# Sums of x for the seven products formed at an attention pair's end, weights kept as float32, and the second half's groups in opposite order

## The chip, the cores and the metric

One core of one Trainium2 chip runs the whole program. The metric is the device time of one execution in microseconds (us); the number shown for a kernel is the median of its runs. The granted clock is the TensorE clock that the profile shows for a stretch, as a fraction of 2.4 GHz.

## The reference

Causal attention for 4 batches and 12 heads (448 positions, head dimension 64), and then a two-layer network on its output, with a squared ReLU between the layers:

```
scores = q @ k.T / sqrt(64); masked above the diagonal; softmax; @ v    # per batch and head
x = attention output as 1792 rows (4 batches x 448) of 768 columns
h = max(x @ w_in, 0)            # 768 x 2048
out = (h * h) @ w_out           # 2048 x 768
```

q, k and v come as float32, the two weights as 64-bit floats.

## The kernel before

**Numbers.** TensorE works on float32 operands in its reduced form, so each operand is kept as two tiles, a high part and a low part (the rest after the high part is taken away), and each product is three matmuls: high x high, high x low, low x high. `split` makes the two parts: a copy for the high part (POOL or ACT, L299) and a subtraction for the low part (DVE or POOL, L301). A weight arrives as 64-bit words; `piece` (L497) loads 128 rows into one of three `raw` buffers, builds the float32 value in one of three `z` buffers (two steps on ACT, three on DVE), and splits it into `wi_t` (w_in) or `late["wo"]` (w_out).

**Stages.** Attention runs in 24 pairs of heads. Pairs 0 to 11 (batches 0 and 1) come first, and their results are split straight into `x_t`. Then the network runs on these 896 rows; meanwhile pairs 12 to 23 (batches 2 and 3) go through attention one after the other on the `a` buffers, and each result goes from PSUM to a buffer of pool `r` and on to DRAM (`x_dram`, L460 to L467). The second half of the network then works on batches 2 and 3.

**The network.** The 2048 columns of w_in come in `NG` = 4 groups. Per group: an h stretch (x times the group's part of w_in, ReLU, square, split into `g_t`) and an o stretch (g times the group's part of w_out), in which 14 output tiles are added up over the groups in `acc` (L764 to L769) and written out in the last group (L770). In the first half the h stretch is done directly (`h_unit`). Each group's two weight parts are also stored, both of the split parts, in DRAM (`keep`, L477: `wi_split`, two stores per row block; `wo_split`), for use in the second half.

**The second half** does each h stretch with seven products in place of eight (`h_pair`, L681). x and w are seen as 2 x 2 blocks. The x side needs, for each of three row blocks i, x11, x21, x22 and the sums t1 = x12 - x11, t2 = x22 - t1, t3 = x22 - x12 and t4 = x21 - t2; x11 and x21 are the two column halves of batch 2, x12 and x22 those of batch 3. `x_parts` (L589) loads the four blocks of one i from `x_dram` into four buffers of pool `f` (L594), makes the four sums with `combine` (DVE or POOL, L287 or L291), and splits all seven results into 21 tiles (L599 to L600). Nine of these tiles lie where attention's buffers were (free at `attended`), twelve in `x_t` (free at `entered`, when the first half's last h stretch is done). They are handed out i by i, while the products take them in the order of `SEVEN`: x11 of i = 0, 1, 2, then t2 of i = 0, 1, 2, then x21, t3, t1, t4, x22.

The w side (`w_parts`, L622) fetches, for each half u of a group, the split parts of three blocks and adds them to whole values (`whole`, L635 or L637), fetches the two parts of the fourth and adds them (L658), makes four sums (`made`), and splits these (`done`). The three blocks that need no sum are used as fetched. Each group's w_out parts come back with `fetch` (L490), eight loads of 384 KB that write the high and low tiles directly.

**What sets the order.** `Plan` is a list scheduler that runs when the program is built. Each operation has a rank, one or more ways (an engine, an estimated duration, the instruction), operations it needs, and the buffers it takes and gives back. `emit` (L97) steps through a simulated time: of all operations that are ready and whose buffer is free, it issues the one that can start first, and the rank only breaks ties; where an operation has several ways it takes the engine on which it would end first. All engines get their instructions in that planned order and execute them in order, SP's DMA issues too. So every wait on the chip is where the chip differs from the plan.

Of the kernel before, what the change touches and what calls it, by code (L numbers as in the profile page):

```python
# [163 lines left out]
def kernel(  # L164
# [17 lines left out]
    nc = tc.nc  # L182
# [73 lines left out]
    plan.pool("r", tiles("r", NR, [P, S], F32), r=2, xs=2, y=6)  # L256
    plan.pool("f", [], fz=5, s=3, xp=4)
# [50 lines left out]
    def attention(s, n, at):  # L308
# [144 lines left out]
        if n < NA:  # L453
            x = x_t[n]
            plan.op(at, [on_act(S, lambda: x[:, 0], lambda: av.t[:, :S], True)],
                    [av], [(("x", n), 0)])
            plan.op(at, [on_dve(S, lambda: x[:, 1], lambda: av.t[:, :S],
                                lambda: x[:, 0].bitcast(F32), ALU.subtract)],
                    [av, (("x", n), 0)], [(("x", n), 1)], drop=[av])
        else:  # L460
            xs = Hold("r", "xs")
# [4 lines left out]
            plan.op(at, [(DMA, 0.7, lambda: nc.sync.dma_start(out=x_dram[n - NA], in_=xs.t))],  # L466
                    [xs], [("xd", n - NA)], drop=[xs])  # L467

# [3 lines left out]
    wo_dram = nc.dram_tensor("wo_split", (NG, 2 * GF, P, 2, CH), F32, kind="Internal").ap()  # L472

    def wo_part(a, ch):
        return late["wo"][:, :, a, ch * CH:(ch + 1) * CH].bitcast(F32)

    def keep(rank, kind, gr, a, ch, after):  # L477
        if kind == "i":
            def go():
                for i in range(2):  # L480
                    nc.sync.dma_start(
                        out=wi_dram[gr, :, a // CB, :, i, a % CB].rearrange("f p n -> p f n"),
                        in_=wi_t[:, i, a].bitcast(F32).rearrange("p (f n) -> p f n", n=P))
            plan.op(rank, [(DMA, 1.9, go)], [(("wi", a), 0), (("wi", a), 1)], [("wid", gr, a)], after)
            return
        plan.op(rank, [(DMA, 1.7, lambda: nc.sync.dma_start(
            out=wo_dram[gr, a + GF * ch], in_=wo_part(a, ch)))],
            [(("wo", a, ch), 0), (("wo", a, ch), 1)], [("wod", gr, a, ch)])

    def fetch(rank, gr, a, ch):  # L490
        plan.op(rank, [(DMA, 1.7, lambda: nc.sync.dma_start(
            out=wo_part(a, ch), in_=wo_dram[gr, a + GF * ch]))],
            [("wod", gr, a, ch)], [(("wo", a, ch), 0), (("wo", a, ch), 1)])
# [3 lines left out]
    def piece(rank, kind, gr, a, ch, after):  # L497
# [40 lines left out]
        split(rank, n, lambda: dst(0), lambda: dst(1), zf, [zt], key, after, [zt])  # L538
        pieces.extend(plan.ops[mark:])
# [41 lines left out]
    x7, owned = {}, {}  # L581
# [7 lines left out]
    def x_parts(i, rank, after):  # L589

        B = {}
        for m, (key, n) in enumerate((("11", i), ("12", NP + i), ("22", NP + CB + i), ("21", CB + i))):
            B[key] = h = Hold("f", "xp")
            plan.op(rank - 6 + m, [(DMA, 0.9, lambda h=h, n=n: nc.sync.dma_start(out=h.t, in_=x_dram[n]))],  # L594
                    [("xd", n)], [h], take=h)

        def done(key):
            t = x7[key, i]
            split(rank, S, lambda: t()[:, 0], lambda: t()[:, 1], lambda: B[key].t, [B[key]],  # L599
                  ("x7", key, i), [after[owned[key, i]]], [B[key]])  # L600
        B["t1"], B["t2"] = Hold("r", "xs"), Hold("r", "xs")
        combine(rank, S, B["t1"], B["12"], B["11"], ALU.subtract, [B["12"], B["11"]], [B["t1"]],
                after=[attended], take=B["t1"], drop=[B["11"]])
        done("11")
        combine(rank, S, B["t2"], B["22"], B["t1"], ALU.subtract, [B["22"], B["t1"]], [B["t2"]],
                take=B["t2"], drop=[B["t1"], B["22"]])
        done("t2")
        done("21")
        B["t3"] = B["12"]
        combine(rank, S, B["12"], B["22"], B["12"], ALU.subtract, [B["22"]], [B["12"]],  # L610
                drop=[B["22"]])
        done("t3")
        done("t1")
        B["t4"] = B["21"]
        combine(rank, S, B["21"], B["21"], B["t2"], ALU.subtract, [B["t2"]], [B["21"]],
                drop=[B["t2"]])
        done("t4")
        done("22")
# [3 lines left out]
    def w_parts(gr, u, rank, last):  # L622
# [22 lines left out]
        for m, (key, f, j) in enumerate((("11", 0, 0), ("22", 1, 1), ("12", 0, 1))):  # L645
            W[key] = w = Hold("w", "w")
            r, src, saved = fetched(m, f, j)
            plan.op(r, [(DMA, 1.2, lambda w=w, src=src: nc.sync.dma_start(out=w.t.bitcast(F32), in_=src))],
                    saved, [(w, 0), (w, 1)], gate, take=w)
            whole(key, lambda w=w: flat(w.t[:, 0].bitcast(F32)), lambda w=w: flat(w.t[:, 1].bitcast(F32)),  # L650
                  [(w, 0), (w, 1)], [w])
        pair = [Hold("f", "fz"), Hold("f", "fz")]
        r, src, saved = fetched(3, 1, 0)
        for i, h in enumerate(pair):
            plan.op(r, [(DMA, 0.7, lambda h=h, i=i: nc.sync.dma_start(
                out=h.t[:, :CBW].rearrange("p (c n) -> p c n", n=P), in_=src[:, i]))], saved, [h], gate, take=h)
        Z["21"] = pair[0]
        combine(rank, CBW, pair[0], pair[0], pair[1], ALU.add, [pair[1]], [pair[0]], drop=[pair[1]])  # L658
# [8 lines left out]
        def made(key, a, b, op, drop):  # L667
            combine(rank, CBW, Z[key], Z[a], Z[b], op, [Z[a], Z[b]], [Z[key]],
                    take=Z[key] if key != "s3" else None, drop=[Z[d] for d in drop])
        made("s1", "21", "22", ALU.add, ("22",))  # L670
        made("s2", "s1", "11", ALU.subtract, ("s1", "11"))
        done("s2")
        made("s3", "11", "21", ALU.subtract, ("11",))
        done("s3")
        done("s1")
        made("s4", "12", "s2", ALU.subtract, ("12", "s2"))
# [63 lines left out]
    def o_unit(ph, gr, t, ch, rank, step, after):  # L740
# [23 lines left out]
        if gr == 0:  # L764
# [4 lines left out]
        plan.op(rank, ways, [ps], [("acc", t, ch)], after if gr == 0 else (), drop=[ps])  # L769
        if gr == NG - 1:  # L770
# [80 lines left out]
    keys = [(key, i) for key in ("11", "t2", "21", "t3", "t1", "t4", "22") for i in range(CB)]  # L851
    for i, key in enumerate(sorted(keys, key=lambda k: k[1])):
        x7[key] = ((lambda i=i: late["x"][i]) if i < NX else (lambda i=i: x_t[i - NX]))
        owned[key] = i >= NX
    for i in range(CB):
        x_parts(i, begin + (rank - begin) * (i + 0.5) / CB, [attended, entered])
    for ph in range(1, NPH):
        for gr in range(NG):
            begin, rank = group(ph, gr, rank, 1.0, begin)
# [33 lines left out]
```

## Time and profile before

| | |
|---|---|
| median of 3 runs | 632.28 us (631.47 to 632.42) |
| the profiled execution's own time | 631.39 us |
| its span, first to last instruction | 629.6 us |
| granted clock, mean | 0.989 |
| busy: TensorE / POOL / DVE / ACT | 604.6 / 371.8 / 367.3 / 325.2 us |
| moved by DMA | 103.77 MB, mean 165 GB/s |

The profiled execution is 1.8 us longer than its span, which is what lies before the first and after the last instruction. A matmul's record is longer than the distance to the next one, because matmuls are pipelined, so TensorE's busy time says where it idled but not how fast it went; for that the granted clock and the number of matmuls in a stretch are needed. Engines other than TensorE cost time only where TensorE waits for them.

### The profile page before, as it was taken

The numbers are of one execution on the slowest core, as the hardware profiler recorded it, in microseconds if no ns is written. First come the engines' busy times: TensorE is split into PE (matmuls) and PEld (weight loads), VectorE is DVE, ScalarE is ACT, GpSimd is POOL, SyncE is SP. The second block draws the span as 40 slices with busy tenths as digits, with TensorE's granted clock in tenths as the row PEclk, the third lists the DMA queues.
The fourth block names the chain that finished last, engine by engine and source line by source line (L and its number), as shares of the span: only waits on it lengthen the run. The fifth ranks groups of instructions, "written<-read, shape, count | busy, mean of one in ns | idle before, by whom it ended". The sixth has DMA issues, their size and how long they took to land.

```text
span 629.6 us, 11242 instructions
## 1 busy us (share of the span) xinstructions
PE 604.6 (96%) x3864; PEld 532.2 (85%) x3864; DVE 367.3 (58%) x822; ACT 325.2 (52%) x803; POOL 371.8 (59%) x454
## 2 busy tenths in 40 slices
PE   4989999999999899999999999799999999999997
PEld 2656677898888798898898889799999999999997
DVE  5679976386767788767874219944015424533222
ACT  4679896865687646587556433345235003302400
POOL 2456766644767763787846459989238706914510
PEclk9799999999999899999999999999999999999999
DMA  9877852797897899886964144873234234333022
GB/s 146 164 187 132 180 122 56 170 324 260 217 258 227 230 256 275 228 251 177 257 199 156 50 129 154 280 223 101 100 110 141 82 126 145 101 101 102 1 89 87
DMA packets 175225, 103.77 MB, mean 165 GB/s; under 512 B 115264, under 2 KB 164928, under 8 KB 175168
## 3 DMA queue, kind: packets, MB, share of 16 engines
q1 hardware_dynamic: 171456, 102.59, 58.9%
q10 hardware_dynamic: 3712, 0.46, 0.5%
q8 instruction: 30, 0.49, 0.3%
q14 instruction: 27, 0.22, 0.1%
HBM read 69.60 MB, written 33.42 MB: 164 GB/s over the span
## 4 chain that ended last, share of the span: by engine, by line
PE 60%; DVE 4%; issue 1%; DMA 1%; POOL 0%; ACT 0%; DVEq 0%; ACTq 0%
PE ps L754 9%; PE ps L756 9%; PE ps L755 9%; PE ps L693 5%; PE ps L695 5%; PE ps L697 5%; PE ps L559 3%; PE ps L561 3%; PE ps L560 3%; PE ps L417 2%; PE ps L397 2%; PE ps L357 2%; DVE x L287 1%; DVE acc L287 1%; DVE words L287 1%
## 5 line engine op out<-in xcount | busy, mean ns | idle before, releaser
L756 PE MATMUL ps<-wo,g 128*128 128x384 f32 x448 | 150.4, 336 | 2.5 <-POOL g L291 2.5
L754 PE MATMUL ps<-wo,g 128*128 128x384 f32 x448 | 152.4, 340 | 0.0
L755 PE MATMUL ps<-wo,g 128*128 128x384 f32 x448 | 150.3, 336 | 0.0
L383 POOL TENSOR_SCALAR ap<-ap,asm 128x64 f32<-128x64 f32 (+6 forms) x120 | 73.9, 636 | 43.6 <-DVE asm L442 22.2
L287 DVE TENSOR_TENSOR acc<-ps,acc 128x384 f32<-128x384 f32 x84 | 46.1, 553 | 84.1 <-PE ps L756 70.5
L284 ACT ACTIVATE r<-ps 128x448 f32<-128x448 f32 x60 | 32.8, 546 | 107.5 <-PE ps L697 79.3
L756 PEld LDWEIGHTS ps<-wo,g 128*128 128x128 f32 x448 | 84.4, 188 | 2.8 <-POOL g L291 2.8
L754 PEld LDWEIGHTS ps<-wo,g 128*128 128x128 f32 x448 | 84.5, 189 | 1.3 <-issue 0.8
L370 DVE CUSTOM_DVE_ANT_0 ps<-ps,mask 128x448 f32<-128x448 f32 (+6 forms) x168 | 68.7, 443 | 27.5 <-PE ps L357 18.3
L755 PEld LDWEIGHTS ps<-wo,g 128*128 128x128 f32 x448 | 84.6, 189 | 0.2
L284 ACT ACTIVATE words<-words 128x384 f32<-128x384 f32 (+3 forms) x112 | 64.5, 614 | 25.7 <-DMA words<-in_moe_w_in_dram 8.6
L559 PE MATMUL ps<-x,wi 128*128 128x448 f32 x192 | 74.4, 387 | 0.3 <-DVE x L287 0.3
L561 PE MATMUL ps<-x,wi 128*128 128x448 f32 x192 | 70.3, 366 | 0.9 <-POOL wi L291 0.9
L560 PE MATMUL ps<-x,wi 128*128 128x448 f32 x192 | 70.2, 365 | 0.0
L374 ACT ACTIVATE ap<-ps,mx 128x448 f32<-128x448 f32 (+6 forms) x126 | 58.7, 483 | 21.3 <-DVE mx L370 15.6
L287 DVE TENSOR_TENSOR r<-ps,r 128x448 f32<-128x448 f32 x40 | 24.9, 623 | 73.7 <-PE ps L697 71.1
L294 POOL TENSOR_SCALAR wi<-words 128x512 fp32r<-128x512 f32 (+1 forms) x27 | 15.9, 589 | 85.1 <-PE ps L695 57.2
L291 POOL TENSOR_TENSOR g<-r,g 128x448 fp32r<-128x448 f32 x50 | 59.5, 1195 | 5.5 <-ACT g L284 2.7
L284 ACT ACTIVATE r<-r 128x448 f32<-128x448 f32 x76 | 43.9, 577 | 21.8 <-DVE r L287 20.4
L693 PE MATMUL ps<-x,wi 128*128 128x448 f32 x138 | 51.3, 372 | 3.7 <-ACT r L284 3.7
L291 POOL TENSOR_TENSOR wi<-words,wi 128x512 fp32r<-128x512 f32 (+1 forms) x41 | 52.3, 1279 | 1.7
L695 PE MATMUL ps<-x,wi 128*128 128x448 f32 x138 | 51.2, 371 | 0.0
(94 smaller groups left out, 1157.4 us busy)
## 6 DMA issues: line engine op xcount, KB each, us to landing
words<-in_moe_w_in_dram SPq DMA_DIRECT2D x24, 512.0 KB, 4.8
words<-in_moe_w_out_dram SPq DMA_DIRECT2D x32, 384.0 KB, 4.1
wi_split<-wi SPq DMA_DIRECT2D x48, 256.0 KB, 3.6
wo_split<-wo SPq DMA_DIRECT2D x32, 384.0 KB, 3.9
wo<-wo_split SPq DMA_DIRECT2D x32, 384.0 KB, 5.1
wi<-wi_split SPq DMA_DIRECT2D x18, 384.0 KB, 3.5
out_dram<-acc SPq DMA_DIRECT2D x28, 192.0 KB, 1.9
v<-in_v_dram SPq DMA_DIRECT2D x24, 192.0 KB, 4.6
```

The lines of the kernel that those rows point to most:

```text
L284: return (ACT, t_act(n, psum, more), lambda: nc.scalar.activation(dst(), src(), func, **kw))
L287: return (DVE, t_dve(n) + more, lambda: nc.vector.tensor_tensor(out=dst(), in0=a(), in1=b(), op=op))
L291: lambda: nc.gpsimd.tensor_tensor(out=dst(), in0=a(), in1=b(), op=op))
L383: (POOL, 0.0005 * CW[c] + 0.34, lambda: nc.gpsimd.tensor_scalar(*operands(), 1.0, op0=ALU.mult, op1=ALU.mult)),
L559: nc.tensor.matmul(o, w[:, 0], x[:, 0], start=c == 0, stop=False)
L560: nc.tensor.matmul(o, w[:, 0], x[:, 1], start=False, stop=False)
L561: nc.tensor.matmul(o, w[:, 1], x[:, 0], start=False, stop=c == NP - 1)
L693: nc.tensor.matmul(o, w.t[:, 0, c], x[:, 0], start=begin and c == 0, stop=False, skip_group_check=True)
L695: nc.tensor.matmul(o, w.t[:, 0, c], x[:, 1], start=False, stop=False, skip_group_check=True)
L754: nc.tensor.matmul(res(), g[:, 0], w[:, 0], start=f == 0, stop=False)
L755: nc.tensor.matmul(res(), g[:, 0], w[:, 1], start=False, stop=False)
L756: nc.tensor.matmul(res(), g[:, 1], w[:, 0], start=False, stop=f == GF - 1)
```

## The change

Four things change together.

1. The sums t1 to t4 are no longer made in `x_parts` from blocks loaded back. A new function `spill` is called when a pair's attention ends. For batch 3 it has loaded the earlier blocks ahead of time into buffers of pool `r` (kind `xs`, now 4 of them), and subtracts them from the attention result while that is still in PSUM: t1 for the first three column blocks; t2, t3 and t4 for the other three. The sums are stored in a new DRAM tensor `xt_dram`. As before, x itself is stored too.
2. `x_part` takes the place of `x_parts`: each of the 21 tiles is one load (three buffers of kind `xp`, before four) and one split, and the tiles are handed out in the order in which the products take them.
3. The second half takes the groups in the order 3, 2, 1, 0. Group 3's w_out parts are still in place from the first half, so nothing is fetched for them. Its outputs are added up in that order and written out with group 0.
4. Weights are kept as float32. `piece` stores the `z` buffer itself: w_out of groups 0 to 2 (196 KB in place of 393 KB each), w_in of groups 1 to 3 (`wz_dram`). The split parts of w_in are kept for groups 0 and 3 alone. `fetch` now loads into a buffer of kind `fo` and splits. `w_parts` differs by group: group 0 as before; group 3 fetches the split parts of the three direct blocks and, beside them, four float32 blocks for its sums; groups 1 and 2 fetch four float32 blocks and split three of them for direct use.

```diff
-    plan.pool("r", tiles("r", NR, [P, S], F32), r=2, xs=2, y=6)
-    plan.pool("f", [], fz=5, s=3, xp=4)
+    plan.pool("r", tiles("r", NR, [P, S], F32), r=2, xs=4, y=6)
+    plan.pool("f", [], fz=5, s=3, xp=3, fo=2)
...
+    def spill(n, av, at):
+        b, c = divmod(n, NP)
+        gate, mark = list(last_sums), len(plan.ops)
...
+        def loaded(place, key):
+            h = Hold("r", "xs")
+            plan.op(at - 8, [(DMA, 0.9, lambda: nc.sync.dma_start(out=h.t, in_=place))],
+                    [key], [h], gate, take=h)
+            return h
+        def less(h, drop):
+            plan.op(at, [(DVE, t_dve(S) + 0.05, lambda: nc.vector.tensor_tensor(
+                out=h.t, in0=result(), in1=h.t, op=ALU.subtract))], [av], [h], drop=drop)
...
+        if second and c < CB:
+            h = loaded(x_dram[c], ("xd", c))
+            less(h, [av])
+            stored(h, *t_place(1))
+        elif second:
+            t1 = loaded(*t_place(1))
+            x21 = loaded(x_dram[c], ("xd", c))
+            x12 = loaded(x_dram[n - CB], ("xd", n - CB))
+            less(t1, [av])
             plan.op(at, [
-                on_act(S, lambda: xs.t, lambda: av.t[:, :S], True),
-                (DVE, t_dve(S) + 0.05, lambda: nc.vector.tensor_copy(xs.t, av.t[:, :S])),
-            ], [av], [xs], take=xs, drop=[av])
...
+                (DVE, t_dve(S) + 0.4, lambda: nc.vector.tensor_tensor(
+                    out=x21.t, in0=x21.t, in1=t1.t, op=ALU.subtract)),
+                (POOL, t_pool(S, True), lambda: nc.gpsimd.tensor_tensor(
+                    out=x21.t, in0=x21.t, in1=t1.t, op=ALU.subtract))], [t1], [x21])
+            less(x12, [av])
+            stored(t1, *t_place(2))
+            stored(x12, *t_place(3))
+            stored(x21, *t_place(4))
+        xs = Hold("r", "xs")
+        plan.op(at, [
+            on_act(S, lambda: xs.t, result, True),
+            (DVE, t_dve(S) + 0.05, lambda: nc.vector.tensor_copy(xs.t, result())),
+        ], [av], [xs], take=xs, drop=[av])
+        last_sums[:] = plan.ops[mark:]
+        stored(xs, x_dram[n], ("xd", n))
...
     def fetch(rank, gr, a, ch):
-        plan.op(rank, [(DMA, 1.7, lambda: nc.sync.dma_start(
-            out=wo_part(a, ch), in_=wo_dram[gr, a + GF * ch]))],
-            [("wod", gr, a, ch)], [(("wo", a, ch), 0), (("wo", a, ch), 1)])
+        h = Hold("f", "fo")
+        plan.op(rank - 6, [(DMA, 0.9, lambda: nc.sync.dma_start(
+            out=h.t[:, :CH], in_=wo_dram[gr, a + GF * ch]))], [("wod", gr, a, ch)], [h], take=h)
+        cols = slice(ch * CH, (ch + 1) * CH)
+        split(rank - 2, CH, lambda: late["wo"][:, 0, a, cols], lambda: late["wo"][:, 1, a, cols],
+              lambda: h.t[:, :CH], [h], ("wo", a, ch), drop=[h])
...
         split(rank, n, lambda: dst(0), lambda: dst(1), zf, [zt], key, after, [zt])
+        if kind == "o" and gr < NG - 1:
+            plan.op(rank, [(DMA, 0.8, lambda: nc.sync.dma_start(out=wo_dram[gr, a + GF * ch], in_=zf()))],
+                    [zt], [("wod", gr, a, ch)], drop=[zt])
+        if kind == "i" and gr > 0:
+            plan.op(rank, [(DMA, 1.0, lambda: nc.sync.dma_start(
+                out=wz_dram[gr, :, a // CB, :, a % CB].rearrange("f p n -> p f n"),
+                in_=zf().rearrange("p (f n) -> p f n", n=P)))],
+                [zt], [("wzd", gr, a)], drop=[zt])
...
-    def x_parts(i, rank, after):
...
+    def x_part(key, i, rank, after):
+        t, h = x7[key, i], Hold("f", "xp")
+        if key[0] == "t":
+            k = int(key[1])
+            place, saved = xt_dram[k - 1, i], ("xt", k, i)
+        else:
+            n = {"11": 0, "21": CB, "22": NP + CB}[key] + i
+            place, saved = x_dram[n], ("xd", n)
+        plan.op(rank - 4, [(DMA, 0.9, lambda: nc.sync.dma_start(out=h.t, in_=place))], [saved], [h], take=h)
+        split(rank, S, lambda: t()[:, 0], lambda: t()[:, 1], lambda: h.t, [h], ("x7", key, i), [after], [h])
...
-        for m, (key, f, j) in enumerate((("11", 0, 0), ("22", 1, 1), ("12", 0, 1))):
+        for m, (key, f, j) in enumerate((("11", 0, 0), ("12", 0, 1), ("22", 1, 1))):
+            if gr not in (0, NG - 1):
+                continue
...
+            if gr == 0:
+                whole(key, lambda w=w: flat(w.t[:, 0].bitcast(F32)), lambda w=w: flat(w.t[:, 1].bitcast(F32)),
+                      [(w, 0), (w, 1)], [w])
...
+        else:
+            for m, (key, f, j) in enumerate((("21", 1, 0), ("22", 1, 1), ("11", 0, 0), ("12", 0, 1))):
+                Z[key] = h = Hold("f", "fz")
+                plan.op(rank - 10 + m, [(DMA, 0.7, lambda h=h, f=f, j=j: nc.sync.dma_start(
+                    out=h.t[:, :CBW].rearrange("p (c n) -> p c n", n=P), in_=wz_dram[gr, 2 * u + f, j]))],
+                    [("wzd", gr, CB * j + c) for c in range(CB)], [h], gate, take=h)
...
+        def direct(key):
+            if gr not in (0, NG - 1):
+                done(key)
...
                 piece(at, "i", gr, c, 0, ())
-                keep(at + 4, "i", gr, c, 0, swap)
+                if gr in (0, NG - 1):
+                    keep(at + 4, gr, c, swap)
...
                 piece(at, "o", gr, i % GF, i // GF, swap)
-                keep(at + 2, "o", gr, i % GF, i // GF, ())
-            else:
+            elif gr < NG - 1:
                 fetch(at, gr, i % GF, i // GF)
...
-    keys = [(key, i) for key in ("11", "t2", "21", "t3", "t1", "t4", "22") for i in range(CB)]
-    for i, key in enumerate(sorted(keys, key=lambda k: k[1])):
...
+    keys = [(OTHER[key], i) for key in SEVEN for i in range(CB)]
+    for m, key in enumerate(keys):
+        x7[key] = ((lambda m=m: late["x"][m]) if m < NX else (lambda m=m: x_t[m - NX]))
+        x_part(*key, begin + (rank - begin) * (m + 0.5) / len(keys), attended if m < NX else entered)
     for ph in range(1, NPH):
-        for gr in range(NG):
+        for gr in range(NG - 1, -1, -1):
             begin, rank = group(ph, gr, rank, 1.0, begin)
```

## Rows read from the trace of the kernel before

**Rows 1.** Engines by stretch, whole span: length, busy us (instructions), clock, DMA.

```profile
0.00:100.00 100.00, 85.68 (x724) 57.44 (x726) 78.32 (x258) 78.54 (x236) 55.33 (x102) 0.97 0.78 153
100.00:371.50 271.50, 268.08 (x1801) 233.35 (x1797) 179.18 (x415) 173.20 (x432) 170.34 (x209) 0.99 0.74 209
371.50:401.30 29.80, 29.80 (x173) 29.75 (x172) 26.55 (x29) 10.59 (x22) 27.92 (x22) 1.00 0.61 201
401.30:412.00 10.70, 7.03 (x27) 5.98 (x26) 10.21 (x12) 4.50 (x10) 9.42 (x8) 0.84 0.73 225
412.00:629.60 217.60, 214.02 (x1149) 205.65 (x1147) 73.02 (x110) 58.36 (x108) 108.76 (x116) 1.00 0.34 107
```

**Rows 2.** TensorE's waits, whole span: us in total, times, longest us.

```profile
PE ps L693 <- ACT r L284: 3.7, 1, 3.7
...
PE ps L756 <- POOL g L291: 2.5, 1, 2.5
...
PE ps L561 <- POOL wi L291: 0.9, 1, 0.9
```

**Rows 3.** The stretches around the second half's first products, as rows 1.

```profile
404.55:408.18 3.63, 0.00 (x0) 0.00 (x0) 3.63 (x4) 1.51 (x5) 3.52 (x4) 1.00 0.82 229
408.18:411.80 3.62, 3.62 (x10) 3.22 (x11) 3.33 (x4) 1.21 (x3) 2.45 (x3) 0.54 0.59 200
411.80:420.00 8.20, 8.20 (x41) 7.53 (x41) 3.12 (x5) 4.59 (x10) 7.89 (x10) 1.00 0.92 273
```

**Rows 4.** ACT in order of time: start us, us, ... [idle before <-releaser].

```profile
406.71 0.58 ACT L284 ACTIVATE x<-r 128x448 fp32r<-128x448 f32 x1 [2.12 <-DVE r L287]
...
407.61 0.52 ACT L284 ACTIVATE r<-ps 128x448 f32<-128x448 f32 x1
```

**Rows 5.** The stretches around TensorE's first-half wait, as rows 1.

```profile
210.30:212.80 2.50, 0.06 (x1) 0.00 (x0) 1.50 (x3) 1.89 (x4) 2.50 (x3) 1.00 0.97 340
212.80:217.20 4.40, 4.36 (x21) 4.25 (x21) 2.65 (x5) 2.22 (x4) 1.67 (x2) 0.62 0.91 261
```

**Rows 6.** Groups by form, 372 to 412 us: xcount, busy us, mean ns, idle.

```profile
L287 DVE TENSOR_TENSOR x<-words,x 128x448 fp32r<-128x448 f32 x9 | 10.7, 1215 | 0.0
...
L637 POOL TENSOR_TENSOR words<-wi 128x384 f32<-128x384 f32 x4 | 5.2, 1304 | 0.0
...
L637 POOL TENSOR_TENSOR words<-w 128x384 f32<-128x384 f32 x2 | 2.8, 1398 | 0.0
...
L287 DVE TENSOR_TENSOR r<-words 128x448 f32<-128x448 f32 x2 | 2.2, 1096 | 0.0
...
L287 DVE TENSOR_TENSOR words<-words 128x448 f32<-128x448 f32 x1 | 1.6, 1571 | 0.0
```

**Rows 7.** Loads of x_dram (L594, 12 in the whole span).

```profile
L594 SPq DMA_DIRECT2D words<-x_dram x12: 372/426/600, 343.2 to 400.2; - x12
...
DMA to landing us min/median/max: 2.5/3.3/5.5
```

**Rows 8.** Group of instructions, the page, whole span: DVE adding from PSUM.

```profile
L287 DVE TENSOR_TENSOR r<-ps,r 128x448 f32<-128x448 f32 x40 | 24.9, 623 | 73.7 <-PE ps L697 71.1
```

**Rows 9.** One 128x512 piece: z taken on ACT, ready and last read on DVE.

```profile
201.38 0.67 ACT L284 ACTIVATE words<-words 128x512 f32<-128x512 f32 x1
...
208.28 0.85 DVE L535 SCALAR_TENSOR_TENSOR words<-words 128x512 int32<-128x512 int32 x1
...
210.42 0.68 DVE L287 TENSOR_TENSOR wi<-words,wi 128x512 fp32r<-128x512 f32 x1
```

**Rows 10.** DMA issues, 120 to 330 us: KB each, median us to landing.

```profile
wo_split<-wo SPq DMA_DIRECT2D x28, 384.0 KB, 4.1
words<-in_moe_w_out_dram SPq DMA_DIRECT2D x26, 384.0 KB, 4.2
words<-in_moe_w_in_dram SPq DMA_DIRECT2D x18, 512.0 KB, 4.6
```

**Rows 11.** DVE's L287 in the second half, 425 to 600 us: ns min/median/max.

```profile
L287 DVE TENSOR_TENSOR words<-words x8: 548/962/1368, 427.1 to 553.5; 128x384 f32<-128x384 f32 x8
```

More of the change, by code (lines that the diff above doesn't have):

```diff
@@ L460, in attention @@
         else:
[L461 to L467 removed]
+            spill(n - NA, av, at)
+    xt_dram = nc.dram_tensor("xt_dram", (4, CB, P, S), F32, kind="Internal").ap()
@@ new lines, with result, stored, t_place @@
+    last_sums = []
+    def spill(n, av, at):
+        b, c = divmod(n, NP)
+        gate, mark = list(last_sums), len(plan.ops)
+        def result():
+            return av.t[:, :S]
+        def stored(h, place, key):
+            plan.op(at, [(DMA, 0.7, lambda: nc.sync.dma_start(out=place, in_=h.t))], [h], [key], drop=[h])
+        def loaded(place, key):
[6 more added lines that the diff above has]
+                out=h.t, in0=result(), in1=h.t, op=ALU.subtract))], [av], [h], drop=drop)
+        def t_place(k):
+            return xt_dram[k - 1, c % CB], ("xt", k, c % CB)
+        second = b == 1
+        if second and c < CB:
[7 more added lines that the diff above has]
+            less(t1, [av])
+            plan.op(at, [
+                (DVE, t_dve(S) + 0.4, lambda: nc.vector.tensor_tensor(
[13 more added lines that the diff above has]
+        stored(xs, x_dram[n], ("xd", n))
@@ L490, in fetch, with keep, go @@
-    def fetch(rank, gr, a, ch):
-        plan.op(rank, [(DMA, 1.7, lambda: nc.sync.dma_start(
-            out=wo_part(a, ch), in_=wo_dram[gr, a + GF * ch]))],
-            [("wod", gr, a, ch)], [(("wo", a, ch), 0), (("wo", a, ch), 1)])
+    wo_dram = nc.dram_tensor("wo_whole", (NG, 2 * GF, P, CH), F32, kind="Internal").ap()
+    wz_dram = nc.dram_tensor("wi_whole", (NG, GF, 2, P, CB, P), F32, kind="Internal").ap()
+    def keep(rank, gr, a, after):
+        def go():
+            for i in range(2):
+                nc.sync.dma_start(
+                    out=wi_dram[gr, :, a // CB, :, i, a % CB].rearrange("f p n -> p f n"),
+                    in_=wi_t[:, i, a].bitcast(F32).rearrange("p (f n) -> p f n", n=P))
+        plan.op(rank, [(DMA, 1.9, go)], [(("wi", a), 0), (("wi", a), 1)], [("wid", gr, a)], after)
@@ L649, in w_parts @@
                     saved, [(w, 0), (w, 1)], gate, take=w)
[L650 to L658, printed above, removed]
+            if gr == 0:
+                whole(key, lambda w=w: flat(w.t[:, 0].bitcast(F32)), lambda w=w: flat(w.t[:, 1].bitcast(F32)),
+                      [(w, 0), (w, 1)], [w])
+        if gr == 0:
+            pair = [Hold("f", "fz"), Hold("f", "fz")]
+            r, src, saved = fetched(3, 1, 0)
+            for i, h in enumerate(pair):
+                plan.op(r, [(DMA, 0.7, lambda h=h, i=i: nc.sync.dma_start(
+                    out=h.t[:, :CBW].rearrange("p (c n) -> p c n", n=P), in_=src[:, i]))], saved, [h], gate, take=h)
+            Z["21"] = pair[0]
+            combine(rank, CBW, pair[0], pair[0], pair[1], ALU.add, [pair[1]], [pair[0]], drop=[pair[1]])
+        else:
[4 more added lines that the diff above has]
+                    [("wzd", gr, CB * j + c) for c in range(CB)], [h], gate, take=h)
         Z["s1"], Z["s2"], Z["s4"] = Hold("f", "s"), Hold("f", "s"), Hold("f", "s")
@@ L763, in o_unit @@
             rank += step
-        if gr == 0:
+        first, final = (0, NG - 1) if ph == 0 else (NG - 1, 0)
+        if gr == first:
             ways = [on_act(CH, acc, res, True),
@@ L768, in o_unit @@
             ways = [on_dve(CH, acc, res, acc, ALU.add)]
-        plan.op(rank, ways, [ps], [("acc", t, ch)], after if gr == 0 else (), drop=[ps])
-        if gr == NG - 1:
+        plan.op(rank, ways, [ps], [("acc", t, ch)], after if gr == first else (), drop=[ps])
+        if gr == final:
             rows = slice(ph * T + t * P, ph * T + (t + 1) * P)
```

50 lines of the change are left out of this document (4 added, 46 removed).

## The prediction, made before the result was known

> **What bounds the kernel now.** I read the stretches of the span first, then TensorE's waits, then the one place that the change aims at.
>
> By stretch [rows 1] TensorE is busy all but 14.3 us of the first 100 us, all but 3.4 us of the next 271.5, all of the 29.8 us of the last o stretch of the first half, 7.03 of the next 10.7 us, and then all but 3.6 us to the end, which are the tail after the last matmul. DVE and POOL are far from full in the second half (73.0 and 108.8 of 217.6 us). So TensorE's own work is the bound, and only its idle time and its slow clock can be won. After the first 100 us, whose order the change hardly touches, TensorE waits three times [rows 2]: 3.7 us for ACT at the second half's start, 2.5 us for POOL in the first half, 0.9 us for POOL.
>
> The first wait is at the hand-over [rows 3]. From 404.55 to 408.18 no matmul runs. From 408.18 to 411.80 the granted clock is 0.54, nearly all at 1.2 GHz, and 10 matmuls take 3.62 us; from 411.80 41 of them take 8.20 us, 0.20 us each, at 2.4 GHz. So the wait costs 3.63 us and the clock behind it 10 x (0.362 - 0.200) = 1.6 us: 5.2 us together.
>
> What TensorE waits for is ACT's copy of the first product out of PSUM at 407.61. ACT works in order, and ahead of the copy it stood 2.12 us for DVE's sum of x whose high part it makes at 406.71 [rows 4]; the copy could have run when the product was done. The sums t1 to t4 of the last row block are what is late. The two engines that make them are full: in the 40.5 us from 371.5 to 412 DVE and POOL are busy 26.55 + 27.92 + 10.21 + 9.42 = 74.1 of 81.0 us [rows 1].
>
> The second wait shows the same price elsewhere [rows 5]: 2.5 us idle, then 4.40 us at a clock of 0.62, which loses 4.40 x 0.38 = 1.7 us: 4.2 us.
>
> **The change, part by part.**
>
> *Sums leave the hand-over.* Twelve sums stand there, seven on DVE and five on POOL; the shortest form takes 1.096 and the longest 1.571 us [rows 6]. At the middle, 1.33, they are 16.0 us (13.2 to 18.9). They go.
>
> *Group 3 first.* Its float32 blocks need no high-plus-low sum: of these, six on POOL cost 5.2 + 2.8 = 8.0 us in this stretch [rows 6], and two pair sums at the same 1.3 us cost 2.6 us. Eight loads of w_out parts leave SP's queue and the DMA engines there too. Together DVE and POOL lose 26.6 of 74.1 us; 47.5 us are left, 24 us for each of two engines, so their work could end at about 371.5 + 24 = 395.5, before the products begin at 401.3. The tiles also come in the order of use: the first product needs three tiles, where before x11 of the last block was made last.
>
> *x loads.* All 21 tiles now come by a load, through three buffers. The buffers are to be had well before 371.5, since the first load of x stands at 343.2 [rows 7], so three are full when the places of the tiles come free at 371.5. Eighteen follow in six rounds. A round is a load of 3.3 us (2.5 to 5.5), an issue of 0.43 us [rows 7], a high part of about 0.57 us (the ACT row at 406.71 shows 0.58) and a low part of 1.2 us (DVE's mean in this stretch [rows 6]): 5.5 us. The tiles are wanted at 401.3 + 0.2 x 3 x m for the m-th of 21, the last at about 413.5. The first three are worked off by some 374, and 374 + 6 x 5.5 = 407. That leaves 6.5 us. With every load at its longest, 5.5 us, and low parts at the 1.57 of the longest form, a round is 8.1 us and the last tile comes at 422.6, 9 us late. I take no wait, because the median row is nearest to how the loads stand, and keep 9 us as the other end.
>
> *Sums at a pair's end.* Nine subtractions read PSUM and one buffer. The nearest row is DVE adding from PSUM, 0.623 us, in 40 cases [rows 8]: 5.6 us, and three sums of the old kind, 4 us. DVE is busy 179 of 271.5 us there [rows 1]; this lies beside TensorE. The subtraction adds a wait on DVE for its loaded operand, and queued behind it on DVE are the additions into acc and attention's maxima, for which TensorE waits through its PSUM banks. But these loads may go as soon as the pair before is done, and twelve pairs share 271.5 us, so about 20 us ahead of use against a landing of at most 5.5 us [rows 7]. Nothing, and if the cover goes, the difference.
>
> *DMAs of the first half.* SP issues 24 more for the sums (12 loads, 12 stores), 6 fewer for w_in (48 become 24 + 18) and 8 fewer for w_out: 10 more at 0.43 us, 4.3 us in 271.5. In bytes, split w_in loses 6.3 MB, w_out 7.9 MB, float32 w_in adds 4.7 MB and the sums 5.5 MB: 4.0 MB less, while the DMA engines are busy 0.74 of this stretch [rows 1]. I count neither a gain nor a loss; a gain is not excluded.
>
> *z buffers.* A store now reads z, so z comes free only when the store has landed. One piece holds z from 201.38 to 211.10, 9.7 us [rows 9]. The nearest store, w_out's split parts, lands in 4.1 us at twice the size [rows 10]; begun when the value is ready, at 209.1, it lands some 2.5 us after the old release: 12.2 us. Three buffers give a piece each 210 / 44 x 3 = 14.3 us (26 + 18 loads in 210 us [rows 10]). It fits by 2 us on average; queued behind the wait on ACT are ReLU copies and exponentials, with TensorE behind them through two banks. I take nothing, and a stall like that of [rows 5], 4.2 us, as the other end.
>
> *Second half.* Twenty-four w_out blocks are split again: 24 copies on ACT or POOL and 24 subtractions on DVE or POOL. By the row of DVE's subtractions and sums of this size, 0.55 to 1.37 us, median 0.96 [rows 11], these are 23 us on engines busy half the time or less [rows 1]; w_parts adds two operations per half of groups 1 and 2 (8) and saves as many in group 3 beyond the hand-over. It is needed one o stretch ahead, so nothing on the path. The spread of that row, 0.55 to 1.37 for one shape, shows that DVE is slowed when POOL works too. The Trainium skill (SBUF — State Buffer, section "SBUF: two separate sides") says that a DVE operation with two SBUF inputs and a GpSimd operation hold a shared port pair by turns, each for its whole length. By that rule the two engines' work adds up, 181.8 of 217.6 us now and about 205 with the change, which would leave few gaps; what this gives is the third rival.
>
> *The sum.* 631.39 - 3.63 - 1.6 = 626.2 for an execution like the profiled one, which stands 0.9 us under the median of 632.28. Set against the median: **627.0 us**.
>
> **The rivals.**
>
> 1. *The loads of x set the pace* (slower side). For: SP's queue is in order, with stores of outputs that wait for DVE between the loads, and only three buffers. It begins to cost when a round is over (413.5 - 374) / 6 = 6.6 us, and decides, so that the whole gain of 5.2 us is gone, at about 7.2 us: late by 3.6 us, and 1.6 us for the clock behind it. At 8.1 us a round it gives 627.0 + 9 + 1.6 = 637.6. Against: the median load gives 5.5.
> 2. *The first-half wait goes too.* The order from 100 us on is planned anew, DMA is lighter, and POOL's wait need not come back: 627.0 - 4.2 = 622.8. Against: the added stores and sums make other coincidences.
> 3. *The second half's new splits become a wait.* At each of three borders from h to o stretch TensorE waits for one copy and one subtraction, 0.6 + 1.0, so 4.8 us: 631.8. For: the spread of [rows 11]. Against: no wait of TensorE there now, and ACT busy only 58.4 of 217.6 us [rows 1].
> 4. *A new wait in the first half*, by ACT standing for z: 627.0 + 4.2 = 631.2.
>
> That the change doesn't do what it says is not a case: the sums, and the fetch for group 3, are gone from the code of the hand-over.
>
> **How the numbers follow.** The forecast has 0.50, rival 1 0.14, rival 2 0.15, rival 3 0.09, rival 4 0.12. Its own range is 624.5 to 629.5. A measurement can tell about 0.2%, 1.3 us, from no change. Faster takes the forecast, rival 2, and the cheaper ends of 3 and 4: 0.70; the middle of rivals 1, 3 and 4 falls within 0.2%: 0.14; the rest is slower: 0.16. For 8 in 10 the range goes from 622.5 (rival 2) to 633.5, which takes in rivals 3 and 4 and the cheap end of rival 1.
>
> **What would show it.** Right: no wait of TensorE between its last o stretch of the first half and the second product of the second half, a granted clock of 1.00 there, DVE and POOL together below 55 us in those 40 us, subtractions from PSUM near 0.62 us. Wrong: TensorE waiting on ACT or DVE for a tile whose load landed late (rival 1); waits at h to o borders behind w_out subtractions (rival 3); ACT's wait for a store of z followed by one of TensorE (rival 4).

## The result, and the profile after

The changed kernel took 624.37 us (median of 4, 623.35 to 626.44) against 631.88 us for the kernel before (median of 4): a ratio of 0.9889, 95% interval 0.9857 to 0.9921, 7.5 us by the medians. The profiled executions differ by 6.7 us in span, 629.6 to 622.9. On another chip the same two kernels differed by 6.3 us (624.38 against 630.72).

The first view is the changed kernel's stretches (columns as in [rows 1]: the length, then busy us and instructions of TensorE, of its weight loads, of DVE, ACT and POOL, then the clock, the DMA share and GB/s), the second its waits of TensorE from 95 us on (us in total, times, the longest).

```profile
100.00:371.50 271.50, 268.85 (x1808) 234.00 (x1807) 195.87 (x424) 173.28 (x429) 181.90 (x220) 1.00 0.70 192
371.50:412.00 40.50, 40.50 (x224) 39.38 (x223) 24.30 (x32) 12.19 (x24) 35.73 (x38) 1.00 0.85 278
412.00:622.90 210.90, 206.06 (x1108) 197.89 (x1106) 91.81 (x126) 65.10 (x125) 110.61 (x115) 1.00 0.19 59
```

```profile
PE ps L612 <- POOL wi L291: 1.6, 1, 1.6
PE ps L741 <- DVE r L287: 1.5, 2, 0.8
PE ps L397 <- POOL ap L383: 1.0, 1, 1.0
```

Against [rows 1, 2] the hand-over's 3.7 us and the first half's 2.5 us are gone, and with them every fall of the clock after the first 50 us: TensorE is busy in all of 371.5 to 412. New are two waits of 0.75 us for DVE in the second half and one of 1.0 us for POOL at 210.9; the wait for POOL at about 170 us has grown from 0.9 to 1.6 us.

To see where the 6.7 us came from, the span is cut at three matmuls that every version has: the first of the first o stretch, the last of the first half, and the first o matmul of the second half. Before, then after, the stretch from the first cut to the second, and from the second to the third, which I call the hand-over stretch (126 matmuls 0.205 us apart, 25.8 us, if nothing waits; the kernels below in which nothing waits take 25.9, which I call the floor):

```profile
128.16:401.10 272.94, 269.52 (x1768) 240.09 (x1766) 192.03 (x407) 164.00 (x399) 180.39 (x204) 0.99 0.74 217
401.10:431.90 30.80, 27.13 (x126) 24.45 (x125) 20.42 (x26) 15.57 (x30) 27.55 (x26) 0.94 0.65 197
```

```profile
127.56:397.69 270.13, 267.48 (x1764) 237.90 (x1763) 197.22 (x409) 158.40 (x387) 187.74 (x218) 1.00 0.74 209
397.69:424.63 26.94, 26.19 (x129) 23.76 (x128) 20.77 (x24) 14.55 (x29) 23.09 (x24) 1.00 0.47 149
```

Up to the first cut 0.6 us are won, in the first half 2.8, in the hand-over stretch 3.9, and from there to the end 0.6 are lost: 6.7. (Before, three of the 126 matmuls, 0.6 us, ran ahead of the second cut; with them the hand-over gave 4.5 and the first half 2.2.)

The parts that the prediction priced by other rows: the sums from PSUM, and who makes the high parts of x (changed kernel, by line over the span, and by form in 371.5 to 412 us).

```profile
L484 DVE TENSOR_TENSOR r<-ps,r x9: 612/624/626, 202.2 to 369.4; 128x448 f32<-128x448 f32 x9
```

```profile
L294 POOL TENSOR_SCALAR x<-words 128x448 fp32r<-128x448 f32 x10 | 6.9, 700 | 3.2 <-DMA words<-xt_dram 3.0
L284 ACT ACTIVATE x<-words 128x448 fp32r<-128x448 f32 x11 | 6.3, 574 | 21.9 <-DMA words<-xt_dram 21.9
```

### The profile page after: what moved, and what is told of

It reads as the page before. It is cut to its first block, busy times and chain, and to the rows that moved or that the text cites. A ratio compares the mean times of both kernels' runs of the same rounds, so it can differ in the third digit from the quotient of the medians.

```text
span 622.9 us, 11301 instructions
## 1 busy us (share of the span) xinstructions
PE 600.5 (96%) x3864; PEld 529.0 (85%) x3864; DVE 391.9 (63%) x840; ACT 329.9 (53%) x814; POOL 383.8 (62%) x473
## 2 busy tenths in 40 slices
DMA packets 166314, 91.68 MB, mean 147 GB/s; under 512 B 115440, under 2 KB 157552, under 8 KB 166256
## 4 chain that ended last, share of the span: by engine, by line
PE 79%; DVE 7%; POOL 6%; DMA 3%; issue 3%; ACT 1%; SPq 1%; ACTq 0%; DVEq 0%; POOLq 0%
PE ps L802 12%; PE ps L804 12%; PE ps L803 12%; PE ps L417 5%; PE ps L397 5%; PE ps L610 5%; PE ps L357 5%; PE ps L741 5%; PE ps L743 5%; PE ps L745 5%; PE ps L612 4%; PE ps L611 4%; POOL ap L383 3%; DVE ps L370 2%; DMA words<-in_moe_w_in_dram 2%
## 5 line engine op out<-in xcount | busy, mean ns | idle before, releaser
L383 POOL TENSOR_SCALAR ap<-ap,asm 128x448 f32<-128x448 f32 (+6 forms) x121 | 74.0, 630 | 47.2 <-DVE asm L442 31.5
L284 ACT ACTIVATE words<-words 128x384 f32<-128x384 f32 (+3 forms) x112 | 66.8, 613 | 51.1 <-DVE words L287 17.3
L287 DVE TENSOR_TENSOR acc<-ps,acc 128x384 f32<-128x384 f32 x84 | 46.1, 554 | 72.8 <-PE ps L804 72.8
L291 POOL TENSOR_TENSOR g<-r,g 128x448 fp32r<-128x448 f32 x54 | 67.7, 1257 | 4.2 <-ACT g L284 1.5
L294 POOL TENSOR_SCALAR wo<-words 128x384 fp32r<-128x384 f32 x36 | 19.4, 539 | 79.6 <-PE ps L804 57.9
L284 ACT ACTIVATE r<-r 128x448 f32<-128x448 f32 x74 | 42.6, 576 | 28.7 <-DVE r L287 26.3
L291 POOL TENSOR_TENSOR wi<-words,wi 128x384 fp32r<-128x384 f32 (+1 forms) x43 | 54.2, 1264 | 0.9
L284 ACT ACTIVATE r<-ps 128x448 f32<-128x448 f32 x60 | 32.7, 546 | 37.2 <-PE ps L745 13.5
L287 DVE CUSTOM_DVE_ANT_0 words<-words 128x768 uint16<-128x768 uint16 (+1 forms) x56 | 46.5, 831 | 6.9 <-ACT words L284 2.7
```

The costliest lines, as they stand in the source:

```text
L284: return (ACT, t_act(n, psum, more), lambda: nc.scalar.activation(dst(), src(), func, **kw))
L287: return (DVE, t_dve(n) + more, lambda: nc.vector.tensor_tensor(out=dst(), in0=a(), in1=b(), op=op))
L291: lambda: nc.gpsimd.tensor_tensor(out=dst(), in0=a(), in1=b(), op=op))
L383: (POOL, 0.0005 * CW[c] + 0.34, lambda: nc.gpsimd.tensor_scalar(*operands(), 1.0, op0=ALU.mult, op1=ALU.mult)),
```

## Experiments

Two questions were open: which part of the change took the hand-over's wait away, and whether the first half's gain belongs to the change at all. The first four kernels take the change apart. Each kernel is compared with the kernel before on its own chip, whose median there was 629.8, 630.7 or 629.6 us.

**The sums alone.** The kernel before with `spill`, `x_part` and the new tile order:

```diff
-    plan.pool("r", tiles("r", NR, [P, S], F32), r=2, xs=2, y=6)
-    plan.pool("f", [], fz=5, s=3, xp=4)
+    plan.pool("r", tiles("r", NR, [P, S], F32), r=2, xs=4, y=6)
+    plan.pool("f", [], fz=5, s=3, xp=3)
...
-            xs = Hold("r", "xs")
+            spill(n - NA, av, at)
...
```

> The kernel before with the sums at the pair's end and the new tile order alone: groups still 0 to 3, weights still kept split, so the hand-over keeps eight loads of w_out and eight high-plus-low sums (10.6 us of DVE and POOL). If the 16 us of x sums and the tile order were what was late, the wait at the hand-over shrinks from 3.7 us to 1 us or less and the clock stays at 1.00 there: 5.2 us less, about 626.7, or 622 to 624 if the first half's wait goes too. If the weights' sums and loads are what counts, the wait stays at 2 us or more with the clock behind it: 629 to 632.

623.23 us, ratio 0.990 (0.988 to 0.993). Its first half and its hand-over stretch, and TensorE's waits in both:

```profile
126.23:398.59 272.36, 268.74 (x1765) 239.10 (x1764) 189.57 (x408) 162.93 (x397) 185.99 (x215) 0.99 0.81 241
398.59:424.49 25.90, 25.90 (x128) 23.82 (x128) 12.47 (x18) 13.16 (x26) 23.70 (x23) 1.00 0.85 280
```

```profile
PE ps L783 <- POOL g L291: 2.7, 1, 2.7
PE ps L607 <- POOL wi L291: 0.9, 1, 0.9
```

The hand-over stretch is at its floor, 25.90 us, although eight loads of w_out and eight sums of weights are still there. The first half is as long as before, with the same two waits on POOL, one of them at another place. So moving the x sums, with the new tile order, takes the hand-over's wait away, and gives nothing in the first half.

**All but the sums.** The changed kernel with `x_parts` and the old result copy put back:

```diff
-            spill(n - NA, av, at)
+            xs = Hold("r", "xs")
...
-        x_part(*key, begin + (rank - begin) * (m + 0.5) / len(keys), attended if m < NX else entered)
+        x_parts(i, begin + (rank - begin) * (i + 0.5) / CB, [attended, entered])
```

> The changed kernel with the x sums put back into the hand-over (four loads, four sums, seven splits per row block, tiles handed out row block by row block): only the group order and the float32 weights are left of the change. If the x sums were what was late, a wait of 2 to 4 us stays at the hand-over: 627 to 631. If the load on DVE and POOL is all that counts, 74.1 - 10.6 = 63.5 us is left for two engines, which ends some 5 us earlier than before, and the wait of 3.7 us goes: 624 to 627.

628.64 us, ratio 0.998 (0.996 to 1.000). The hand-over stretch:

```profile
399.96:428.60 28.64, 26.66 (x128) 23.52 (x128) 22.17 (x25) 12.71 (x25) 25.30 (x26) 1.00 0.27 84
```

```profile
PE ps L714 <- DVE r L287: 2.0, 2, 1.6
```

With fewer weight sums there the wait shrinks from 3.7 to 2.0 us and no slow clock follows, but 2.7 us over the floor stay. So taking out either load helps: group order and float32 weights, which take weights' sums and loads of w_out out of this stretch, win 2.8 of the 5.5 us over the floor (31.4 with the three early matmuls), the x sums, by the kernel above, all of it. Whether the sums or the loads of the weights made those 2.8 us was not tested.

**Groups in the old order, all else changed.**

```diff
-        for gr in range(NG - 1, -1, -1):
+        for gr in range(NG):
...
-        if kind == "o" and gr < NG - 1:
+        if kind == "o":
...
-            elif gr < NG - 1:
+            else:
```

> The changed kernel with the groups of the second half in the order 0, 1, 2, 3: w_out of all four groups is stored and loaded back (32 in place of 24), and the hand-over has group 0's eight high-plus-low sums (10.6 us of DVE and POOL) and the splits of w_out's first blocks. If the order of groups matters, a wait of 1.5 to 4 us comes back at the hand-over, with or without the clock: 626 to 630. If the x sums alone were the cause, nothing comes back: 624 to 626.

628.91 us, ratio 0.999 (0.997 to 1.001): no gain is left. The hand-over stretch, and POOL's and DVE's work in it from 412 us on (POOL first):

```profile
399.64:429.31 29.67, 26.43 (x129) 23.68 (x129) 25.90 (x27) 19.17 (x38) 29.59 (x27) 1.00 0.55 178
```

```profile
413.03 2.30 POOL L291 TENSOR_TENSOR wo<-words,wo 128x384 fp32r<-128x384 f32 x2
...
419.69 1.34 POOL L291 TENSOR_TENSOR wo<-words,wo 128x384 fp32r<-128x384 f32 x1
```

```profile
421.37 3.60 DVE L287 TENSOR_TENSOR words<-words 128x384 f32<-128x384 f32 x3
424.90 0.61 DVE L287 TENSOR_TENSOR r<-ps,r 128x448 f32<-128x448 f32 x1
425.43 0.96 DVE L287 TENSOR_TENSOR wi<-words,wi 128x384 fp32r<-128x384 f32 x1
```

TensorE waits 3.0 us, to 425.56, for DVE's addition at 424.90, which stands behind three sums of weights. The sums-alone kernel has the same group order and the same eight weight sums and sits at 25.90; what the hand-over has beside it here is more splitting. POOL is full (29.59 of 29.67 us) and DVE twice as busy as there (25.90 against 12.47). The splits of w_out in this stretch, by form:

```profile
L291 POOL TENSOR_TENSOR wo<-words,wo 128x384 fp32r<-128x384 f32 x4 | 4.9, 1243 | 0.0
L287 DVE TENSOR_TENSOR wo<-words,wo 128x384 fp32r<-128x384 f32 x2 | 2.9, 1454 | 1.5 <-POOL wo L294 1.5
L294 POOL TENSOR_SCALAR wo<-words 128x384 fp32r<-128x384 f32 x2 | 1.3, 661 | 0.0
```

These are 9.1 us, and eleven low parts of w_in take 13.9 us on the two engines, where the sums-alone kernel's four take 5.7. The changed kernel has these eleven too (13.5 us); what the reversed order spares it in this stretch is the splits of w_out and some 7 us of weight sums (4.1 against 11.2 us). So float32 weights cost 3.8 us at the hand-over in the old order (29.67 against 25.90) and 1.0 us in the reversed one (26.94 against 25.90, below); with the weights kept split, in the sums-alone kernel, the old order costs nothing. Which part of that added work made the wait was not tested. The hand-over is also not all that this kernel loses: its span is 4.6 us longer than the changed kernel's (627.5 against 622.9), 2.7 in this stretch and 1.6 in the first half, where a slow clock follows a wait of 1.86 us (last section).

**Tiles row block by row block.**

```diff
-    keys = [(OTHER[key], i) for key in SEVEN for i in range(CB)]
+    keys = [(OTHER[key], i) for i in range(CB) for key in SEVEN]
```

> The changed kernel with its 21 tiles loaded row block by row block again, nothing else. In the changed kernel the last tile is ready at 408.5, about when its product comes. If the order of the tiles matters, the first product waits for the third row block's first tile, the fifteenth of 21, at about 400 in place of 399, and each product's last third waits again: 1 to 3 us in all, 625 to 628. If only the work on DVE and POOL matters, the last tile comes at the same 408.5 and the end moves by less than 1 us: 624 to 625.5.

623.78 us, ratio 0.991 (0.989 to 0.994), and a hand-over stretch at the floor:

```profile
399.54:425.42 25.88, 25.88 (x129) 23.83 (x129) 16.68 (x20) 15.49 (x31) 25.54 (x25) 1.00 0.47 155
```

The order of the tiles was worth nothing, although the loads did go out in the other order.

**The changed kernel again, and the sums with reversed groups but split weights,** on one chip. The edit of the second, against the sums alone:

```diff
-        for gr in range(NG):
+        for gr in range(NG - 1, -1, -1):
...
-                keep(at + 2, "o", gr, i % GF, i // GF, ())
-            else:
+                if gr < NG - 1:
+                    keep(at + 2, "o", gr, i % GF, i // GF, ())
+            elif gr < NG - 1:
```

> The changed kernel again, on the same chip as the three kernels beside it, so that it and the sums with reversed groups can be compared without a change of chip. 623 to 626 if the first comparison holds, a ratio of 0.986 to 0.993 to the kernel before.

> The sums at the pair's end and the reversed groups, with the weights kept split as in the kernel before: the float32 weights alone are taken from the change. If these gain nothing (their splits cost DVE and POOL time in the second half, and the 12 MB of DMA that they save hid behind TensorE), this is as fast as the changed kernel or up to 1.5 us faster: 622.5 to 624.5. If the lighter DMA is worth something, it is 1 to 3 us slower than the changed kernel: 625 to 627.

624.38 us (6 runs, 623.59 to 625.46), ratio 0.989 (0.987 to 0.992), and 622.87 us (6 runs, 621.33 to 626.44), ratio 0.988 (0.984 to 0.991). The intervals overlap, so which is faster is not settled; that float32 weights bring a gain is not to be seen. They take DMA from 105.05 MB, in the second of these kernels, to 91.68 MB, and none of TensorE's waits names a transfer. The hand-over stretch without them is at the floor, with them (changed kernel, above) 1.0 us over it:

```profile
398.13:424.03 25.90, 25.90 (x128) 23.82 (x128) 17.53 (x23) 13.48 (x26) 25.02 (x25) 1.00 0.51 161
```

**Fewer load buffers,** two and then one in place of three:

```diff
-    plan.pool("f", [], fz=5, s=3, xp=3, fo=2)
+    plan.pool("f", [], fz=5, s=3, xp=1, fo=2)
```

> The changed kernel with two load buffers for the 21 tiles in place of three. In the changed kernel the last tile was ready at 408.5, some 0.5 us before its product. If the loads set the pace of the tiles, 19 of them now go through two buffers at 5.5 us a round: 374 + 9.5 x 5.5 = 426, a wait of 10 us or more with the clock behind it, 634 to 640. If DVE and POOL set the pace, the loads still come in time and the end moves by less than 2 us: 624 to 626.

> The changed kernel with a single load buffer for the 21 tiles in place of three. With two, no wait came. With one, each tile is a load, an issue, a high and a low part in turn: 20 rounds from 374 on. At 5.5 us a round the last tile comes at 374 + 110 = 484, some 75 us after its product, so the loads must now be the bound: 680 to 710. If the planner's rounds are shorter (2.6 us is the shortest landing: 4.8 us a round), 374 + 96 = 470: 665 to 690.

625.22 us, ratio 0.991 (0.988 to 0.994), with two, and 623.52 us, ratio 0.991 (0.988 to 0.993), with one. With one, the hand-over stretch and a line of SP's queue in it:

```profile
398.34:424.67 26.33, 26.26 (x128) 23.68 (x128) 20.21 (x24) 16.27 (x35) 24.92 (x22) 1.00 0.57 177
```

```profile
399.72 5.21 SPq L649 DMA_DIRECT2D words<-xt_dram  x8
```

TensorE idles 0.07 us there, and eight loads go out within 5.21 us, where one buffer with a landing of 2.3 us or more (3.3 at the median) would let two or three through. So `xp` does not limit the loads in flight. In `emit` a buffer leaves the count as soon as its last reader is planned, not when that reader ends, and the next load takes another of the pool's eleven tiles; as operations are issued by their planned start, the load can stand ahead of that reader. My rounds through three buffers never existed.

**The same kernels in other plans.** The planner's guess for a DMA issue at 1.5 or 1.3 us in place of 1.4, in the kernel before and in the changed one:

```diff
-    ISSUE = 1.4
+    ISSUE = 1.5
```

> The kernel before with the planner's guess for a DMA issue at 1.5 us in place of 1.4. If the hand-over's wait comes from its work on DVE and POOL, it stays here at 2 us or more; the first half's wait of 2.5 us may come elsewhere, or with another length. 628 to 633. If the hand-over's wait was as much a matter of where the plan was off, it may fall under 1 us here: 624 to 628.

> The kernel before with the planner's guess at 1.3 us. As for 1.5: a wait of 2 us or more at the hand-over if the work makes it (628 to 633), under 1 us in one of the two if it is the plan (624 to 628).

> The changed kernel with the planner's guess for a DMA issue at 1.5 us in place of 1.4: the same work, planned into another order. If the first half's waits (1.6 and 1.0 us in the changed kernel, 0.9 and 2.5 us and a slow clock before) come from where the plan happens to be off, they come out differently here, between 0 and 5 us, while the hand-over stays without a wait over 1 us: 622 to 629. If the change itself removed the first half's wait of 2.5 us, they stay as in the changed kernel: 623.5 to 625.5.

> The changed kernel with the planner's guess at 1.3 us. No wait over 1 us at the hand-over if the work decides, and first-half waits that sum to 2 to 4 us wherever they come: 623 to 627. A wait of 2 us or more at the hand-over would say that the plan decides: 626 to 630.

The kernel before: 627.64 us at 1.5 and 627.54 us at 1.3, ratios 0.997 (0.995 to 0.999) and 0.996 (0.994 to 0.998). The changed kernel: 625.35 and 625.31 us, ratios 0.991 (0.988 to 0.994) and 0.992 (0.989 to 0.996). First halves and hand-over stretches of the kernel before, at 1.5 and at 1.3:

```profile
127.71:398.20 270.49, 268.22 (x1767) 238.57 (x1766) 194.69 (x407) 162.42 (x397) 181.90 (x206) 1.00 0.75 219
398.20:428.57 30.37, 26.62 (x125) 22.87 (x125) 21.91 (x28) 13.96 (x26) 28.00 (x28) 1.00 0.62 200
```

```profile
127.56:397.91 270.35, 268.43 (x1768) 238.59 (x1766) 195.53 (x404) 161.89 (x398) 184.96 (x208) 1.00 0.75 218
397.91:428.73 30.82, 27.15 (x126) 24.47 (x125) 19.75 (x26) 15.57 (x30) 27.62 (x27) 0.94 0.61 198
```

and of the changed kernel at 1.5 and at 1.3:

```profile
128.00:399.04 271.04, 267.69 (x1764) 237.88 (x1763) 192.68 (x407) 158.46 (x388) 186.68 (x218) 1.00 0.73 208
399.04:425.95 26.91, 26.15 (x128) 23.76 (x128) 20.80 (x24) 14.78 (x29) 23.11 (x24) 1.00 0.47 151
```

```profile
128.55:398.03 269.48, 267.77 (x1765) 237.98 (x1763) 192.25 (x409) 157.49 (x386) 189.31 (x218) 1.00 0.74 209
398.03:424.92 26.89, 26.15 (x129) 23.75 (x129) 20.79 (x24) 14.78 (x29) 23.23 (x24) 1.00 0.47 150
```

The hand-over stretch hardly moves with the plan: 30.4 to 30.8 us in three plans of the kernel before, 26.9 in three of the changed one. At 1.5 the kernel before waits 3.7 us there as well, but in pieces, and its clock stays at 1.00:

```profile
PE ps L695 <- DVE x L287: 2.0, 2, 1.6
PE ps L693 <- ACT r L284: 1.4, 1, 1.4
PE ps L693 <- DVE r L287: 0.3, 1, 0.3
```

The first half does move: the kernel before in another plan has 270.4 us in place of 272.9, as short as the changed kernel's 269.5 to 271.0. So the hand-over's gain is the change's, and the first half's 2.2 us is a plan of the kernel before that happened to be worse.

The size of the whole gain moves with it. With the same guess in both kernels the change is worth 2.2 us at 1.3 (627.54 to 625.31, on one chip) and about 3.4 us at 1.5 (by the two ratios, from two chips); the profiled spans differ by 3.1 us in both (626.5 to 623.4 and 626.7 to 623.6), where they differ by 6.7 us at 1.4. The hand-over gives 3.9 and 3.5 us in these two; at 1.3, 1.0 us of it is lost again before the first cut and 0.7 after the third. So about half of the gain first measured depends on the plan. The kernels that take the change apart ran in one plan each, and their first halves go from 270.2 to 272.4 us: their total times carry such differences too, and what they show of the cause is read from their hand-over stretches.

## Why the prediction was right

The forecast was 627.0 us (own range 624.5 to 629.5, full range 622.5 to 633.5); 624.37 came out. The sum had one term, the hand-over, and that came nearly as forecast, for the reason given. The rest of the gain comes from no term of it: of the 6.7 us between the spans, 2.2 lie in the first half and 0.6 before it, and 0.6 are lost again at the end. The first half's part is the plan's, by the kernels at 1.5 and 1.3, and there the whole change is worth 2.2 and 3.4 us, less than the 5.2 forecast. So the mechanism was right, and that the total fell within the own range owes something to luck.

- *The hand-over, 5.2 us.* Right in mechanism, a little large. 4.5 us were won there. 0.75 us of the rest is one of the new waits for DVE. The clock stayed at 1.00, as forecast, and the 1.6 us behind the wait went with it.
- *DVE and POOL together below 55 us in those 40.* This sign did not come; mis-sized: 24.30 + 35.73 = 60.0 us, 12.5 over the 47.5 of the sum. It left out that the planner may move the high parts of x from ACT to POOL; it moved ten, 6.9 us. Most of the rest is the second half's own work, which stands in this window because its products now begin 3.4 us earlier and don't wait: additions from PSUM and parts of g take 8.0 us in it, against 1.2 before. By form in 371.5 to 412 us, the changed kernel:

```profile
L291 POOL TENSOR_TENSOR g<-r,g 128x448 fp32r<-128x448 f32 x3 | 3.8, 1259 | 0.1
L287 DVE TENSOR_TENSOR r<-ps,r 128x448 f32<-128x448 f32 x5 | 3.1, 616 | 2.2 <-PE ps L745 2.2
L294 POOL TENSOR_SCALAR g<-r 128x448 fp32r<-128x448 f32 x2 | 1.1, 564 | 0.0
```

- *Order of the tiles.* Wrong as a reason: handing them out row block by row block costs nothing.
- *Eight loads of w_out less.* They were not what was late either: the sums-alone kernel keeps them and sits at the floor. The reversed order earns its place only together with float32 weights.
- *x loads in six rounds of 5.5 us, and rival 1.* The step "through three buffers" failed: the number is not a limit on loads in flight, and even one costs nothing. The rival's 0.14 was for a mechanism that the planner does not have, which its code could have told.
- *Sums from PSUM, 0.623 us each.* Right: nine at a median of 0.624 us, beside TensorE's work.
- *z buffers, rival 4.* ACT did wait for the stores, 8 times for w_out (6.6 us in all, the longest 2.5) and 4 times for w_in (2.5 us in all):

```profile
ACT words L284 <- DMA wo_whole<-words: 6.6, 8, 2.5
...
ACT words L284 <- DMA wi_whole<-words: 2.5, 4, 1.2
```

  In none of its waits after the first 100 us did TensorE stand for ACT.
- *Second half, rival 3.* No waits at the borders of h and o stretches, but two of 0.75 us inside h stretches, for DVE additions from PSUM; I had counted nothing. From the third cut to the end 0.6 us are lost.
- *The Trainium skill's rule* (SBUF — State Buffer, section "SBUF: two separate sides"), by which DVE operations with two SBUF inputs and GpSimd operations take turns. The prediction's sum for it, 205 of 217.6 us, was wrong in what it added: it took all of DVE's work, and much of that reads PSUM. After 412 us DVE and POOL are busy 91.81 + 110.61 = 202.4 of 210.9 us, and 44.9 of them are these:

```profile
L287 DVE TENSOR_TENSOR acc<-ps,acc 128x384 f32<-128x384 f32 x42 | 23.2, 557 | 57.0 <-PE ps L804 57.0
L287 DVE TENSOR_TENSOR r<-ps,r 128x448 f32<-128x448 f32 x35 | 21.7, 621 | 32.1 <-PE ps L745 32.1
```

  That leaves 157.5 us, and TensorE waited 1.5 us there. Nor is a sum of recorded busy times a limit: in the kernel with the groups in the old order the two engines add up to 25.90 + 29.59 = 55.5 us in a hand-over stretch of 29.67 us. What the traces of the two kernels show after 100 us is how long DVE's additions and subtractions of 128x448 take. With two SBUF operands they took 0.61 to 0.62 us in the five cases with no POOL work beside them and 0.61 to 1.57 us in the 45 cases beside POOL's work; with one operand in PSUM they took 0.61 to 0.63 us in all 95 cases. That agrees with the rule; that the two engines in fact took turns is not tested by any run here.
- *Rival 2.* It came true in part: the first half's 2.5 us wait and the slow clock behind it (4.2 us) went, and a wait grew by 0.6. But it was not the change that did it: at the two other guesses the kernel before itself has a wait of 1.2 and of 1.1 us in its place, with no slow clock behind it (1.00).

## What to carry to other kernels

When a planner fixes the order of all engines, run the kernel before in two or three neighbouring plans first: the part of a difference that moves with the plan, here about half of 7 us, is not the change's. What lasts is work taken out of the one stretch where helpers are full and TensorE is about to need their results; here 12 sums moved from two full engines to an earlier place, nine of them reading PSUM there, took away a wait that stood in three plans. The DMA bytes saved brought nothing that could be measured here, where none of TensorE's waits names a transfer, and the work that saves them (splitting again) has to be hidden on its own.

## What the runs showed of the hardware that I had not expected

The length of a wait alone did not tell whether TensorE's clock fell behind it. In the kernel with tiles by row block, TensorE idled 1.92 us up to 171.23, and from 172 to 180 the granted clock was 0.81; in the changed kernel it idled 1.56 us at the same place and the clock stayed at 1.00; with the groups in the old order it idled 3.00 us up to 425.56 and the clock stayed at 1.00 as well. The kernels with the groups in the old order and with one load buffer idled 1.86 and 1.84 us at 171 us and ran at 0.81 and 0.82 from 172 to 180. At another place, near 299 us, the sums-alone kernel idled 2.69 us and ran the next 2 us at 0.50, and the sums with reversed groups idled 2.15 us and kept 1.00. The rows behind the wait at 171 us, the row-block kernel first, the changed kernel second:

```profile
172.00:180.00 8.00, 8.00 (x59) 6.16 (x59) 6.57 (x16) 5.14 (x11) 5.26 (x6) 0.81 0.73 193
```

```profile
170.40:180.00 9.60, 9.55 (x78) 7.47 (x79) 8.40 (x18) 6.89 (x16) 6.02 (x7) 1.00 0.73 190
```

So the price of a wait of 2 to 3 us is uncertain by the 1.5 to 1.7 us of slow clock that may follow it (8.00 x 0.19 = 1.5 in the first of these rows), which is more than many of the differences measured here.
